# V of a cache group as one load into two neighbouring pages, used behind its own group's K

## The chip, the cores and the metric

The kernel runs on one core of a Trainium2 chip. The metric is the device time of one execution in microseconds (us), the median of several runs. The core has five engines that run side by side and wait for each other through semaphores: TensorE (PE in the profile, its weight loads PEld), VectorE (DVE), ScalarE (ACT), GpSimd (POOL) and SyncE (SP). Here SP issues all large loads, in order, on one queue that is served by 16 DMA engines. On-chip memory has 128 partitions; matmul results go to a separate memory (PSUM, tiles named ps... here).

## What is computed

One decode step: attention of one new token over a long cache (A), a gated feed-forward layer (B), and a gate that mixes them. Cut to what matters, in bf16:

```
Hq, Hkv, Sk, Dh = 32, 8, 32768, 128        # x: (1, 1, 512)
g = sigmoid((x * gate_w).sum(-1))
q = (x @ wq)                               # 32 heads, 4 for each of the 8 K/V groups
scores = q . k * Dh**-0.5                  # 32768 scores for each head
p = softmax(scores);  o = p . v;  a = o @ wo
b = (silu(x @ w_gate) * (x @ w_up)) @ w_down      # inner width 1792
out = g * a + (1 - g) * b
```

The cache is the work: 8 groups of K and V with 32768 rows of 128 bf16 numbers, 8.39 MB each for K and for V, 134 MB in all. Each byte is used once, for 4 heads.

## The kernel before, in words

**Pages.** The cache passes through `page`, five pages of 32 KB per partition (4.19 MB over 128 partitions). A page holds one block: half of K or of V of one group, 16384 rows, 128 to a partition. K block b uses page `PG_K[b]` = 0 or 2, V block b uses `PG_V[b]` = 1 or 3 (L71, L72). Page 4 (`PG_X`) holds wq at the start and wo at the end; page 3 (`PG_F`) first holds the weights w_gate and w_up.

**Loads** (SP, L298 to L348). SP waits until a page is free and issues its load; everything behind it on SP waits too. The order is wq, x, gate_w, w_gate, w_up, K(0,0), K(0,1), V(0,0), K(1,0), V(0,1), K(1,1), and then for each group g from 2 on K(g,0), V(g-1,0), K(g,1), V(g-1,1). So V comes one group after K. A K page is free when TensorE has transposed it (`sem_fill`), a V page when its matmuls are done (`sem_v_free`). V(0,1) waits until the products with w_gate and w_up are done (`sem_pe_h`). At the end come V(7,0), V(7,1), which goes into K's page 0 (L342) so that it need not wait for V(6,1), then w_down in one load and wo in five cuts (8, 10, 8, 4 and 2 of 32 columns).

**TensorE** (L351 on). The loop at L500 runs over nine values of i = 16 g, the last for the V that is left. For a block of K (`emit_k`) it waits for the page and works through eight units. A unit is eight transposes of 128 x 128 fp32 words (`emit_fill`, L408), which VectorE copies back to on-chip memory as ktT (L630), and, two units later, 16 small matmuls that make scores (`emit_scores`, L420). For a block of V (`emit_v`, L465) it waits for the page and for the exps of that block, and does 32 matmuls of 16 columns (4 rows by 4 heads) by 512, spread over four strips of 32 columns of the array, into `ps_o`. The order in one pass is K(g,0), a reduce, V(g-1,0), K(g,1), V(g-1,1). The reduce (`emit_reduce`, L446) sums the strips of the group before that one, out of `acc`.

**The other engines.** When both K blocks of a group are through, VectorE has its maximum over the partition (L635, L637), GpSimd takes it over all partitions (L293), and ScalarE makes the bias (L526) and eight exps (L535, four heads by two blocks) into ET. ScalarE then copies the group before out of `ps_o` into `acc` (L547). ET, `ps_o` and `acc` are single buffers.

**The end** (`emit_end`, L474 to L498, and L673 to L691). Sum of the exps (L477), the last reduce, eight of 14 matmuls with w_down (L205 in `emit_wide`), then o in the shape for wo (L659 to L671), the first cut of wo (L205, eight matmuls), the rest of w_down (six), the second cut (ten), a copy by VectorE (L685), the rest of wo as small matmuls (L217 in `emit_rows`), a copy (L687) and two stores (L244).

Of the kernel before, what the change touches and what calls it, by code (L numbers as in the profile page):

```python
# [13 lines left out]
def bass_gated_mix__gqa_block_cached__swiglu_ffn__decode_kernel(  # L14
# [14 lines left out]
    G = A_k_cache.shape[1]  # L29
# [3 lines left out]
    HPG = H // G  # L33
# [36 lines left out]

    PG_K = (0, 2)  # L71
    PG_V = (1, 3)  # L72
    PG_F = 3
    PG_X = 4
    NPG = 5

    with ExitStack() as es:
        def S_(name):
            return es.enter_context(nc.semaphore(name))

        sem_page = [S_(f"s_page{i}") for i in range(4)]
        sem_q = S_("s_q")
# [112 lines left out]

        def row_view(p):
            return page[:, p, :].rearrange("p (r d) -> p r d", d=DH)

        wq_v = page[:, PG_X, 0 : KC * H * DH].rearrange("p (c n) -> p c n", c=KC)
        wgu = page[:, PG_F, 0 : 2 * KC * F].rearrange("p (w c f) -> p w c f", w=2, c=KC)  # L200
        wo_v = page[:, PG_X, 0 : WOJ * NOUT].rearrange("p (j n) -> p j n", j=WOJ)
# [47 lines left out]
        with nc.Block("main") as block:  # L249
# [47 lines left out]
            @block.sync  # L297
            def _(sp):  # L298
                def cache(which, g, b, p, sem):
                    sp.dma_start(  # L300
                        page[:, p, :].rearrange("p (r d) -> p r d", d=DH),
                        which[0, g, b * BLK : (b + 1) * BLK, :].rearrange("(p r) d -> p r d", r=R),
                    ).then_inc(sem, 16)

                def load_k(g, b):
                    if g:
                        sp.wait_ge(sem_fill, UPG * (g - 1) + UPP * (b + 1))
                    cache(A_k_cache, g, b, PG_K[b], sem_page[PG_K[b]])

                def load_v(g, b):  # L310
                    if g:
                        sp.wait_ge(sem_v_free, NB * (g - 1) + b + 1)
                    elif PG_V[b] == PG_F:
                        sp.wait_ge(sem_pe_h, 1)
                    cache(A_v_cache, g, b, PG_V[b], sem_page[PG_V[b]])

                sp.dma_start(wq_v, A_wq.rearrange("(p c) n -> p c n", c=KC)).then_inc(sem_q, 16)  # L317
                sp.dma_start(x_row[0:1, :], A_x[0, :, :]).then_inc(sem_ld_x, 16)
                sp.dma_start(gw_row[0:1, :], gate_w.unsqueeze(0)).then_inc(sem_ld_x, 16)
                for w, src in enumerate((B_w_gate, B_w_up)):  # L320
                    sp.dma_start(  # L321
                        wgu[:, w, :, :], src.rearrange("(p c) f -> p c f", c=KC)
                    ).then_inc(sem_f, 16)
                for b in range(NB):
                    load_k(0, b)
                load_v(0, 0)
                load_k(1, 0)
                load_v(0, 1)
                load_k(1, 1)
                for g in range(2, G):  # L330
                    for b in range(NB):
                        load_k(g, b)
                        load_v(g - 1, b)

                def load_wo(k):
                    a, b = WO_CUTS[k], WO_CUTS[k + 1]
                    src = A_wo.rearrange("(p j) n -> p j n", j=WOJ)
                    sp.dma_start(wo_v[:, a:b, :], src[:, a:b, :]).then_inc(sem_wo[k], 16)  # L338

                load_v(G - 1, 0)  # L340
                sp.wait_ge(sem_fill, UPG * (G - 1) + UPP)
                cache(A_v_cache, G - 1, 1, PG_K[0], sem_page[PG_K[0]])  # L342
                sp.dma_start(  # L343
                    wd[:, :, :], B_w_down.rearrange("(p j) n -> p j n", j=FC)
                ).then_inc(sem_ld_wd, 16)
                sp.wait_ge(sem_pe_q, 1)
                for k in range(len(sem_wo)):
                    load_wo(k)  # L348

            @block.tensor  # L350
            def _(pe):  # L351
# [77 lines left out]
                def emit_k(i, b):  # L429
                    pe.wait_ge(sem_page[PG_K[b]], i + 16)  # L430
                    for u in range(UPP + LAG):
                        if u >= LAG:
                            pe.wait_ge(sem_cp, i + (UPP * b + u - LAG + 1))
                        if u < UPP:
                            emit_fill(b, u)
                        if u >= LAG:
                            if u == LAG:
                                pe.wait_ge(sem_exp, i + 8 * (b + 1))
                            ins = emit_scores(b, u - LAG)
                    ins.then_inc(sem_sc, 8)  # L440

                def emit_reduce(i):
                    pe.wait_ge(sem_acc, i)
                    pe.wait_ge(sem_rc, i)
                    for q in range(RQ):
# [8 lines left out]

                def emit_v(i, b, pg=None, landed=None):
                    pg = PG_V[b] if pg is None else pg
                    view = row_view(pg)
                    if b == 0:
                        emit_reduce(i)
                    pe.wait_ge(sem_page[pg], i if landed is None else landed)  # L460
                    pe.wait_ge(sem_exp, i + 8 * (b + 1))
                    for k in range(R // RQ):
                        n = b * R + k * RQ
                        c = k % NSTRIP
                        ins = pe.matmul(  # L465
                            ps_o[32 * c : 32 * c + RQ * HPG, :],
                            ET[:, n : n + RQ, :].rearrange("p n h -> p (n h)"),
                            view[:, k * RQ : (k + 1) * RQ, :],
                            start=(b == 0 and k < NSTRIP),
                            stop=(b == NB - 1 and k >= R // RQ - NSTRIP),  # L470
                            skip_group_check=True,
                        )
                    ins.then_inc(sem_v_free, 1)

                def emit_end():
# [7 lines left out]
                    ).then_inc(sem_pe_S, 1)  # L483
                    emit_reduce((G + 1) * STEP)
                    pe.wait_ge(sem_dve_tT, 1)
# [13 lines left out]

                with pe.Fori(0, (G + 1) * STEP, STEP) as i:  # L500
                    for b in range(NB):
                        with pe.If(i < G * STEP):
                            emit_k(i, b)
                            if b:
                                with pe.If(i > 0):
                                    emit_v(i, b)
                        if b == 0:
                            with pe.If(i > 0):
                                emit_v(i, b)
                    with pe.If(i > (G - 1) * STEP):  # L510
                        emit_v(G * STEP, 1, PG_K[0], (G + 1) * STEP)
                        emit_end()

            @block.scalar
            def _(act):
# [8 lines left out]
                def emit_exps(g):  # L524
# [3 lines left out]
                    ).then_inc(sem_nbias, 1)  # L528
                    act.wait_ge(sem_nbias, g + 1)
                    for b in range(NB):  # L530
                        if g:
                            act.wait_ge(sem_v_free, NB * (g - 1) + b + 1)
                        sc = ps_sc[b][:, :].rearrange("p (t h) -> p h t", h=HPG)
# [10 lines left out]
                def emit_acc(g):  # L544
                    act.wait_ge(sem_v_free, NB * (g + 1))
                    act.wait_ge(sem_red, STEP * (g + 1))
# [4 lines left out]
                for g in range(G):  # L551
                    emit_exps(g)
                    if g:
                        emit_acc(g - 1)
                emit_acc(G - 1)

            @block.vector
            def _(dve):
# [8 lines left out]
                dchain(dve.memset(qblk[:, :], 0.0))  # L567
                dve.sem_inc(sem_rc, 2 * STEP)
                dve.wait_ge(sem_pe_x, 1)
# [52 lines left out]
                def copy_red(i, at):  # L622
                    dve.wait_ge(sem_red, i)
                    dve.tensor_copy(oT[:, at], ps_m[:, M_P0 : M_P0 + HPG]).then_inc(sem_rc, STEP)

                with dve.Fori(0, G * STEP, STEP) as i:
# [15 lines left out]
                    )  # L642
                    with dve.If(i > STEP):
                        copy_red(i, bass.ds(i, HPG))

# [4 lines left out]
                dve.memset(ps_w[:, :], 0.0).then_inc(sem_psw, 1)  # L650
                copy_red(G * STEP, slice(G * STEP, G * STEP + HPG))
                dve.wait_ge(sem_pe_S, 1)
# [3 lines left out]
                )  # L656
                copy_red((G + 1) * STEP, slice((G + 1) * STEP, (G + 1) * STEP + HPG))
                dve.wait_ge(sem_rc, STEP * (G + 2))
                dve.tensor_tensor(  # L659
                    oTs[:, :].rearrange("p (g h) -> p g h", h=HPG),  # L660
                    oT[:, 2 * STEP :].rearrange("p (g s) -> p g s", s=STEP)[:, :, 0:HPG],
                    rSg[:, :].rearrange("p (g h) -> p g h", h=HPG),
# [57 lines left out]
```

## Time and profile before

| | us |
|---|---|
| runs, median of 3 (lowest to highest) | 352.46 (352.34 to 352.58) |
| profiled execution, first to last instruction (span) | 350.2 |
| median less span (start and end of an execution) | 2.26 |

| engine | busy us in the span | share |
|---|---|---|
| PE, PEld | 269.0, 230.9 | 77%, 66% |
| DVE | 176.8 | 50% |
| ACT | 32.3 | 9% |
| POOL | 6.9 | 2% |

How to read what follows: a profile page gives, first, such shares; then the span in 40 slices, with a digit for the busy tenths of each slice (9 is 90% or more); then the DMA queues with packets, MB and the share of 16 engines' span that their packets took; then the chain that ended last, which is followed back from the last instruction to what released each step. A row of the timeline has start, length, engine, line, operation, `written<-read`, shape and count, and in brackets the idle time before and what ended it. The granted clock is the share of full speed that TensorE's throttle gave it; its mean over the span is 0.846, and single stretches show 0.50 or 1.00. The page's issue table gives 16 K loads and 16 V loads of 4096 KB, with a median of 27.1 and 31.2 us from issue to landing, nearly all of it spent in the queue behind others.

### The profile page before, as it was taken

To read this page: it belongs to the slowest core of one execution; us is meant where nothing else is said; L and a number is where in the kernel's file an instruction comes from. 1 tells how busy PE (TensorE), PEld (TensorE's weight loads), DVE (VectorE), ACT (ScalarE), POOL (GpSimd) and SP (SyncE) were. 2 spreads that over 40 slices of the span, in tenths; PEclk is the share of its full clock that TensorE was granted. 3 is DMA by queue.
4 is the path that set the end of the run, shared out by engine and by line. 5 is a ranking of instruction groups with operands and counts; after the bars stand their busy time and mean duration, and the time that the engine had idled before them with its cause. 6 is when DMAs were issued, how large, how long until landed. Compare 5 with 4: busy or idle time off the path is not lost.

```text
span 350.2 us, 8919 instructions
## 1 busy us (share of the span) xinstructions
PE 269.0 (77%) x4005; PEld 230.9 (66%) x4005; DVE 176.8 (50%) x193; ACT 32.3 (9%) x148; POOL 6.9 (2%) x29
## 2 busy tenths in 40 slices
PE   0446987799999959897797969694896949795675
PEld 0446987787796939495785839392886849493332
DVE  0111868474783928366382828183473819184011
ACT  1000000500030040002100040004000040004000
POOL 4000000000000000000000000000000000000000
PEclk9999989696998989679696969899698969679565
DMA  8999999999999999999999999999999999999995
GB/s 348 395 453 417 438 445 425 418 419 449 434 430 423 427 446 430 430 423 423 449 430 434 419 434 438 434 430 419 442 438 434 423 423 442 438 434 419 425 415 234
DMA packets 5924, 148.23 MB, mean 423 GB/s; under 512 B 666, under 2 KB 668, under 8 KB 924
## 3 DMA queue, kind: packets, MB, share of 16 engines
q1 hardware_dynamic: 5912, 148.12, 98.6%
q8 instruction: 6, 0.10, 0.1%
q14 instruction: 2, 0.02, 0.0%
q10 hardware_dynamic: 4, 0.00, 0.0%
HBM read 148.11 MB, written 0.00 MB: 423 GB/s over the span
## 4 chain that ended last, share of the span: by engine, by line
DMA 64%; PE 32%; DVE 2%; SPq 1%; issue 1%
DMA page<-in_A_k_cache_dram 53%; PE pst L408 24%; DMA page<-in_A_wo_dram 11%; PE ps_sc L420 5%; DVE ktT L630 1%; PE ps_o L465 1%; PE pst L217 1%; PE pst L205 0%; PE ps_m L446 0%; SPq L321 0%; SPq L300 0%; DVE part L685 0%; SPq L343 0%; SPq L338 0%; SPq L317 0%
## 5 line engine op out<-in xcount | busy, mean ns | idle before, releaser
L630 DVE COPY ktT<-pst 128x2048 bf16<-128x2048 bf16 x128 | 156.1, 1224 | 106.4 <-PE pst L408 99.2
L408 PE MATMUL pst<-ident_f,page 128*128 128x128 f32 x1024 | 158.8, 313 | 40.9 <-DMA page<-in_A_k_cache_dram 35.6
L408 PEld LDWEIGHTS pst<-ident_f,page 128*128 128x128 f32 x1024 | 136.1, 163 | 51.6 <-DMA page<-in_A_k_cache_dram 43.7
L420 PE MATMUL ps_sc<-qcur,ktT 128*128 128x8 bf16 x2048 | 67.8, 166 | 8.6 <-DVE ktT L630 8.6
L420 PEld LDWEIGHTS ps_sc<-qcur,ktT 128*128 128x128 bf16 x2048 | 66.9, 97 | 11.3 <-DVE ktT L630 10.0
L465 PE MATMUL ps_o<-page,ET 128*16 128x512 bf16 x512 | 43.2, 497 | 4.6 <-DMA page<-in_A_v_cache_dram 4.6
L465 PEld LDWEIGHTS ps_o<-page,ET 128*16 128x16 bf16 x512 | 13.5, 105 | 23.8 <-issue 11.9
L526 ACT ACTIVATE nbias<-gmax 128x4 f32<-128x4 f32 x8 | 1.7, 207 | 263.4 <-POOL gmax L293 263.4
L535 ACT ACTIVATE ET<-ps_sc,nbias 128x128 bf16<-128x128 f32 x64 | 24.1, 553 | 0.6
L535 ACT ACTIVATION_READ_ACCUMULATOR ET<-ps_sc,nbias 128x1 f32 x64 | 18.0, 282 | 0.0
L635 DVE TENSOR_REDUCE pmaxf<-ps_sc 128x4 f32<-128x512 f32 x16 | 11.1, 692 | 11.5 <-PE ps_sc L420 11.5
L446 PE MATMUL ps_m<-sel,acc 128*128 128x4 f32 x72 | 10.4, 268 | 3.8 <-ACT acc L547 3.8
L446 PEld LDWEIGHTS ps_m<-sel,acc 128*128 128x128 f32 x72 | 9.8, 211 | 4.4 <-ACT acc L547 4.4
L394 PE MATMUL ps_m<-xT,page 128*128 128x1 bf16 x112 | 6.9, 198 | 5.0 <-DMA page<-in_B_w_up_dram 5.0
L357 PE MATMUL ps_m<-ones_bf,x_row 1*128 1x1 bf16 x4 | 0.3, 172 | 12.9 <-DMA gw_row<-in_gate_w_dram 12.9
L394 PEld LDWEIGHTS ps_m<-xT,page 128*128 128x128 bf16 x112 | 6.8, 159 | 5.1 <-DMA page<-in_B_w_up_dram 5.1
L293 POOL PARTITION_ALL_REDUCE gmax<-pmax x8 | 3.0, 373 | 302.8 <-DVE pmax L637 302.8
L357 PEld LDWEIGHTS ps_m<-ones_bf,x_row 1*128 1x128 bf16 x4 | 0.2, 115 | 12.9 <-DMA gw_row<-in_gate_w_dram 12.9
L547 ACT ACTIVATE acc<-ps_o 128x512 f32<-128x512 f32 x8 | 5.2, 648 | 13.7 <-PE ps_o L465 13.7
L653 DVE RECIPROCAL rS<-pst 128x32 f32<-128x32 f32 x1 | 0.4, 357 | 12.0 <-PE pst L477 12.0
L570 DVE CAST xT<-ps_m 128x4 bf16<-128x4 f32 x1 | 0.2, 162 | 11.8 <-PE ps_m L357 11.8
L609 DVE TENSOR_TENSOR t<-sg,ps_m 128x14 f32<-128x14 f32 x1 | 0.2, 170 | 10.8 <-ACT sg L520 10.8
(65 smaller groups left out, 38.5 us busy)
## 6 DMA issues: line engine op xcount, KB each, us to landing
page<-in_A_k_cache_dram SPq DMA_DIRECT2D x16, 4096.0 KB, 27.1
page<-in_A_v_cache_dram SPq DMA_DIRECT2D x16, 4096.0 KB, 31.2
page<-in_A_wq_dram SPq DMA_DIRECT2D x1, 4096.0 KB, 12.2
page<-in_A_wo_dram SPq DMA_DIRECT2D x2, 1024.0 KB, 38.8
page<-in_B_w_gate_dram SPq DMA_DIRECT2D x1, 1792.0 KB, 15.3
page<-in_B_w_up_dram SPq DMA_DIRECT2D x1, 1792.0 KB, 20.5
wd<-in_B_w_down_dram SPq DMA_DIRECT2D x1, 1792.0 KB, 34.5
page<-in_A_wo_dram SPq DMA_DIRECT2D x1, 1280.0 KB, 39.1
```

What stands on the lines that cost most here:

```text
L217: ins = pe.matmul(ps_c[32 * oc : 32 * oc + (1 if e else SW), 0:128], lhs(e), rhs[:, oc * 128 : (oc + 1) * 128], start=first, stop=last, sk ...
L293: pool.partition_all_reduce(gmax[:, g, :], pmax[:, g * STEP : g * STEP + HPG], 128, ReduceOp.max).then_inc(sem_gmax, 1)
L394: ins = pe.matmul(ps_m[:, base + j : base + j + 1], wgu[:, w, c, :].rearrange("d (p j) -> d j p", j=FC)[:, j, :], xT[:, c : c + 1], start= ...
L408: ins = pe.transpose(pst[u % NST][:, k * 128 : (k + 1) * 128], kv[:, n * 128 : (n + 1) * 128], ident_f[:, :],)
L420: ins = pe.matmul(ps_sc[b][:, col : col + 2 * HPG], kt[:, k, e, :], qcur[:, e, :], start=(e == 0), stop=(e == 1),)
L446: ins = pe.matmul(ps_m[:, M_P0 : M_P0 + HPG], acc[:, q, :], sel4[:, q * HPG : (q + 1) * HPG], start=(q == 0), stop=(q == RQ - 1),)
L465: ins = pe.matmul(ps_o[32 * c : 32 * c + RQ * HPG, :], ET[:, n : n + RQ, :].rearrange("p n h -> p (n h)"), view[:, k * RQ : (k + 1) * RQ, ...
L526: act.activation(nbias[:, g, :], gmax[:, g, :], ACT.Copy, scale=-SCALE).then_inc(sem_nbias, 1)
L535: act.activation(ET[:, b * R : (b + 1) * R, h], sc[:, h, :], ACT.Exp, bias=nbias[:, g, h : h + 1], scale=SCALE, accum_out=esum[:, g, b, h ...
L547: act.activation(acc[:, :, :].rearrange("p q d -> p (q d)"), ps_o[:, :], ACT.Copy).then_inc(sem_acc, STEP)
L630: dve.tensor_copy(ktT[:, u % NKT, :], pst[u % NST][:, :].bitcast(BF16)).then_inc(sem_cp, 1)
L635: dve.tensor_reduce(pmaxf[:, b, :], sc, AX.X, ALU.max).then_inc(sem_pmax, 4)
```

## The change

K's pages become 0 and 1. Pages 2 and 3 become one V buffer of 64 KB per partition, which holds a whole group's V; w_gate and w_up lie at its start first. V of a group is one load of 8.39 MB, issued behind both K loads of the same group, and it waits until the V before has been used up (V of group 0: until w_gate and w_up have). In it a partition holds 256 neighbouring rows. So that scores and V rows stay in step, a K block now takes, of each partition's 256 rows, the first or the second 128: 32 KB out of each 64 KB.

TensorE does K(g,0), K(g,1), reduce of group g-1, V(g) in each of eight passes, with no branches. V waits for all eight exps of its group and is 64 matmuls in a row. ScalarE waits for the V before ahead of all eight exps, and copies `ps_o` to `acc` directly behind a group's exps. VectorE copies the reduce's result in each pass. The end is the same but for the numbering.

The diff, cut to its core:

```diff
-    PG_K = (0, 2)
-    PG_V = (1, 3)
-    PG_F = 3
+    PG_K = (0, 1)
+    PG_V = 2
...
+        v_page = page[:, PG_V : PG_V + NB, :].rearrange("p b e -> p (b e)")
+        v_rows = v_page.rearrange("p (r d) -> p r d", d=DH)
...
                 def load_k(g, b):
                     if g:
                         sp.wait_ge(sem_fill, UPG * (g - 1) + UPP * (b + 1))
-                    cache(A_k_cache, g, b, PG_K[b], sem_page[PG_K[b]])
+                    sp.dma_start(
+                        page[:, PG_K[b], :],
+                        A_k_cache[0, g, :, :].rearrange("(p b r) d -> b p (r d)", b=NB, r=R)[b],
+                    ).then_inc(sem_page[b], 16)
...
+                def load_v(g):
                     if g:
-                        sp.wait_ge(sem_v_free, NB * (g - 1) + b + 1)
-                    elif PG_V[b] == PG_F:
+                        sp.wait_ge(sem_v_free, g)
+                    else:
                         sp.wait_ge(sem_pe_h, 1)
-                    cache(A_v_cache, g, b, PG_V[b], sem_page[PG_V[b]])
+                    sp.dma_start(
+                        v_page, A_v_cache[0, g, :, :].rearrange("(p r) d -> p (r d)", r=NT)
+                    ).then_inc(sem_page[NB], 16)
...
-                for b in range(NB):
-                    load_k(0, b)
-                load_v(0, 0)
-                load_k(1, 0)
-                load_v(0, 1)
-                load_k(1, 1)
-                for g in range(2, G):
+                for g in range(G):
                     for b in range(NB):
                         load_k(g, b)
-                        load_v(g - 1, b)
+                    load_v(g)
...
-                load_v(G - 1, 0)
-                sp.wait_ge(sem_fill, UPG * (G - 1) + UPP)
-                cache(A_v_cache, G - 1, 1, PG_K[0], sem_page[PG_K[0]])
...
+                def emit_v(i):
+                    pe.wait_ge(sem_page[NB], i + 16)
+                    pe.wait_ge(sem_exp, i + 2 * STEP)
+                    for k in range(NT // RQ):
+                        n = k * RQ
...
+                with pe.Fori(0, G * STEP, STEP) as i:
                     for b in range(NB):
...
+                        emit_k(i, b)
+                    emit_reduce(i)
+                    emit_v(i)
+                emit_end()
...
+                    if g:
+                        act.wait_ge(sem_v_free, g)
                     for b in range(NB):
-                        if g:
-                            act.wait_ge(sem_v_free, NB * (g - 1) + b + 1)
...
                 for g in range(G):
                     emit_exps(g)
-                    if g:
-                        emit_acc(g - 1)
-                emit_acc(G - 1)
+                    emit_acc(g)
```

More of the change, by code (lines that the diff above doesn't have):

```diff
@@ L79, in S_ @@
             return es.enter_context(nc.semaphore(name))
-        sem_page = [S_(f"s_page{i}") for i in range(4)]
+        sem_page = [S_(f"s_page{i}") for i in range(3)]
         sem_q = S_("s_q")
@@ L194, in bass_gated_mix__gqa_block_cached__swiglu_ffn__decode_kernel @@
         ps_w = pst[0][:, 512:1024]
-        def row_view(p):
-            return page[:, p, :].rearrange("p (r d) -> p r d", d=DH)
+        v_page = page[:, PG_V : PG_V + NB, :].rearrange("p b e -> p (b e)")
+        v_rows = v_page.rearrange("p (r d) -> p r d", d=DH)
         wq_v = page[:, PG_X, 0 : KC * H * DH].rearrange("p (c n) -> p c n", c=KC)
-        wgu = page[:, PG_F, 0 : 2 * KC * F].rearrange("p (w c f) -> p w c f", w=2, c=KC)
+        wgu = page[:, PG_V, 0 : 2 * KC * F].rearrange("p (w c f) -> p w c f", w=2, c=KC)
         wo_v = page[:, PG_X, 0 : WOJ * NOUT].rearrange("p (j n) -> p j n", j=WOJ)
@@ L298, in _ @@
             def _(sp):
[L299 to L303, printed above, removed]
                 def load_k(g, b):
@@ L307, in load_k @@
                         sp.wait_ge(sem_fill, UPG * (g - 1) + UPP * (b + 1))
-                    cache(A_k_cache, g, b, PG_K[b], sem_page[PG_K[b]])
-                def load_v(g, b):
+                    sp.dma_start(
[3 more added lines that the diff above has]
+                def load_v(g):
                     if g:
-                        sp.wait_ge(sem_v_free, NB * (g - 1) + b + 1)
-                    elif PG_V[b] == PG_F:
+                        sp.wait_ge(sem_v_free, g)
+                    else:
                         sp.wait_ge(sem_pe_h, 1)
-                    cache(A_v_cache, g, b, PG_V[b], sem_page[PG_V[b]])
+                    sp.dma_start(
+                        v_page, A_v_cache[0, g, :, :].rearrange("(p r) d -> p (r d)", r=NT)
+                    ).then_inc(sem_page[NB], 16)
                 sp.dma_start(wq_v, A_wq.rearrange("(p c) n -> p c n", c=KC)).then_inc(sem_q, 16)
@@ L429, in emit_k @@
                 def emit_k(i, b):
-                    pe.wait_ge(sem_page[PG_K[b]], i + 16)
+                    pe.wait_ge(sem_page[b], i + 16)
                     for u in range(UPP + LAG):
@@ L442, in emit_reduce @@
                 def emit_reduce(i):
-                    pe.wait_ge(sem_acc, i)
-                    pe.wait_ge(sem_rc, i)
+                    pe.wait_ge(sem_acc, i + STEP)
+                    pe.wait_ge(sem_rc, i + STEP)
                     for q in range(RQ):
@@ L453, in emit_reduce @@
                     ins.then_inc(sem_red, STEP)
[L455 to L463, printed above, removed]
+                def emit_v(i):
[3 more added lines that the diff above has]
+                        n = k * RQ
                         c = k % NSTRIP
@@ L467, in emit_v @@
                             ET[:, n : n + RQ, :].rearrange("p n h -> p (n h)"),
-                            view[:, k * RQ : (k + 1) * RQ, :],
-                            start=(b == 0 and k < NSTRIP),
-                            stop=(b == NB - 1 and k >= R // RQ - NSTRIP),
+                            v_rows[:, n : n + RQ, :],
+                            start=(k < NSTRIP),
+                            stop=(k >= NT // RQ - NSTRIP),
                             skip_group_check=True,
@@ L483, in emit_end @@
                     ).then_inc(sem_pe_S, 1)
-                    emit_reduce((G + 1) * STEP)
+                    emit_reduce(G * STEP)
                     pe.wait_ge(sem_dve_tT, 1)
@@ L498, in emit_end @@
                         emit_wide(pe, wd, tT, j, False, False)
-                with pe.Fori(0, (G + 1) * STEP, STEP) as i:
+                with pe.Fori(0, G * STEP, STEP) as i:
                     for b in range(NB):
[L502 to L512, printed above, removed]
+                        emit_k(i, b)
+                    emit_reduce(i)
+                    emit_v(i)
+                emit_end()
             @block.scalar
@@ L544, in emit_acc @@
                 def emit_acc(g):
-                    act.wait_ge(sem_v_free, NB * (g + 1))
+                    act.wait_ge(sem_v_free, g + 1)
                     act.wait_ge(sem_red, STEP * (g + 1))
@@ L567, in _ @@
                 dchain(dve.memset(qblk[:, :], 0.0))
-                dve.sem_inc(sem_rc, 2 * STEP)
+                dve.sem_inc(sem_rc, STEP)
                 dve.wait_ge(sem_pe_x, 1)
@@ L622, in copy_red @@
                 def copy_red(i, at):
-                    dve.wait_ge(sem_red, i)
+                    dve.wait_ge(sem_red, i + STEP)
                     dve.tensor_copy(oT[:, at], ps_m[:, M_P0 : M_P0 + HPG]).then_inc(sem_rc, STEP)
@@ L642, in _ @@
                     )
-                    with dve.If(i > STEP):
-                        copy_red(i, bass.ds(i, HPG))
+                    copy_red(i, bass.ds(i, HPG))
                 dve.wait_ge(sem_exp, STEP * (G + 1))
@@ L650, in _ @@
                 dve.memset(ps_w[:, :], 0.0).then_inc(sem_psw, 1)
-                copy_red(G * STEP, slice(G * STEP, G * STEP + HPG))
                 dve.wait_ge(sem_pe_S, 1)
@@ L656, in _ @@
                 )
-                copy_red((G + 1) * STEP, slice((G + 1) * STEP, (G + 1) * STEP + HPG))
+                copy_red(G * STEP, slice(G * STEP, G * STEP + HPG))
                 dve.wait_ge(sem_rc, STEP * (G + 2))
@@ L660, in _ @@
                     oTs[:, :].rearrange("p (g h) -> p g h", h=HPG),
-                    oT[:, 2 * STEP :].rearrange("p (g s) -> p g s", s=STEP)[:, :, 0:HPG],
+                    oT[:, STEP : (G + 1) * STEP].rearrange("p (g s) -> p g s", s=STEP)[:, :, 0:HPG],
                     rSg[:, :].rearrange("p (g h) -> p g h", h=HPG),
```

## The prediction

> **What bounds the kernel now.** I read the page's slices and queue table first, then the chain that ended last, then the timeline of the last 50 us.
>
> ```profile
> DMA  8999999999999999999999999999999999999995
> ...
> q1 hardware_dynamic: 5912, 148.12, 98.6%
> ```
>
> The loads keep the 16 DMA engines busy for 98.6% of the span. The missing 1.4% of 350.2 us is 4.9 us, about what the two ends account for (the first load is issued at 0.74 us, nothing is loaded after 348.1 us). So there is one unbroken stream of 148.12 MB, and nothing between the ends can be won by issuing a load earlier.
>
> The pace of that stream is read where TensorE waits for a K page. These starts are single rows of the timeline (columns: start, length, engine, line, operation; in brackets the idle time before and what ended it):
>
> ```profile
> 246.44 5.38 PE L408 MATMUL pst<-ident_f,page 128*128 128x128 f32 x24 [5.64 <-DMA page<-in_A_k_cache_dram]
> ...
> 304.73 5.38 PE L408 MATMUL pst<-ident_f,page 128*128 128x128 f32 x24 [1.97 <-DMA page<-in_A_k_cache_dram]
> ...
> 318.06 0.56 PE L420 MATMUL ps_sc<-qcur,ktT 128*128 128x8 bf16 x16 [0.54 <-DVE ktT L630]
> 318.54 1.90 PE L465 MATMUL ps_o<-page,ET 128*16 128x512 bf16 x32
> ...
> 323.18 0.30 ACT L535 ACTIVATION_READ_ACCUMULATOR ET<-ps_sc,nbias 128x1 f32 x1
> ...
> 325.64 3.59 PE L465 MATMUL ps_o<-page,ET 128*16 128x512 bf16 x32
> ...
> 333.87 3.59 PE L465 MATMUL ps_o<-page,ET 128*16 128x512 bf16 x32 [4.63 <-DMA page<-in_A_v_cache_dram]
> ...
> 341.17 1.04 PE L205 MATMUL pst<-wd,tT 128*1 128x512 bf16 x6
> 343.74 1.44 PE L205 MATMUL pst<-page,O 128*1 128x512 bf16 x10 [1.54 <-DMA page<-in_A_wo_dram]
> ```
>
> Six pages lie between the K pages that land at 246.4 and 304.7: 58.29 / 6 = 9.715 us for 4.19 MB, or 431.7 GB/s. Three more pages land by 333.83 (29.1 us, the same pace). What is left then is w_down and wo, 6.03 MB, and the chain shows that they set the end:
>
> ```profile
> 304.59 39.11 DMA page<-in_A_wo_dram
> 343.70 0.04 issue
> 343.74 1.46 PE pst L205 x10
> ...
> 348.12 0.43 PE pst L217 x4
> 348.55 0.02 issue
> 348.58 0.29 DVE res_row L687
> ```
>
> So the end is the last byte of wo plus 0.5 us of rows and the store. Ahead of it TensorE has little room: it is ready for wo's second cut at 342.21 (341.17 + 1.04), and that cut lands at 343.70. **The room in the tail is 1.5 us.** That is the number this change has to be held against.
>
> **Part by part.**
>
> *The stream's bytes and order.* The same 32 pages are loaded, in the order K, K, V, V instead of K and V in turn. K of group 7, block 0 is now the 29th page; block 1 was the 29th before, at 304.73. Both leave three pages to come, so V of group 7 is complete at 333.83 as before, w_down and wo as before. This needs the queue never to run dry, which is checked below.
>
> *Pieces of 64 KB.* A V page was 128 pieces of 32 KB; now 128 pieces of 64 KB make two pages. The tail bounds what a piece costs. Its 6.03 MB arrive in 768 pieces (48 per engine) in 348.08 - 333.83 = 14.25 us. At 431.7 GB/s they would take 13.97 us with 11.5 pieces of 32 KB per engine. So 0.28 us / 36.5 = 7.7 ns a piece. V loses 1024 of 2048 pieces, 64 per engine: -0.49 us. If the queue cuts 64 KB into two again, 0. I take -0.43 us, the 7 groups of V ahead of the last K, as nothing shows a cut.
>
> *Half as many V loads.* The queue table leaves no gap to save at a load's start or end (4.9 us over everything, ends included), so I take 0. The Trainium skill ("DMA: Bandwidth & Descriptors", Anatomy of one DMA) gives a fixed 2.0 us for each load beside its bytes. Taken as time of the stream, 8 loads fewer would be an estimated 16 us; here it would make a page 11.6 us, and the rows show 9.715, so loads queued behind each other hide it.
>
> *Where the pages lie in HBM.* K is now 32 KB of every 64 KB, V 64 KB per partition; before, all pages were contiguous, partitions 32 KB apart. No row has this pitch. The nearest is wo, 2 to 10 KB out of every 32 KB, which runs at 6.03 MB / 14.25 us = 423 GB/s, all of it explained by pieces in the line above. I take 0; each 1% of the stream's pace would be 3.1 us (32 x 9.715 / 100). The Trainium skill (same page, Latency and other measured facts) speaks against the change: copies lose speed at power-of-two row pitches, 207 GB/s at 512 KiB where 214 is full. An estimated 3% here would be some 10 us; no run here shows such a pitch, and 64 KB is an eighth of it.
>
> *V follows its own group on TensorE.* This is the costly part. Before, V of group g-1 ran between the K blocks of group g, and its exps had been ready for long; at the end only 32 matmuls waited for the last page. Now each group is serial: K block 0, K block 1, maximum and exps, 64 V matmuls. The pieces, from rows:
> - a K block, start to end of its scores: 11.95 us (227.02 to 238.97, at full clock), 13.05, 13.55, 13.89 (304.73 to 318.62), 14.0 us (246.44 to 260.45). Directly behind another K block there is one row: 46.15 to 59.79, 13.64 us, 0.70 of them "issue". I take 13.5 for block 0 and 13.0 for block 1; bounds 11.95 and 13.9.
> - scores to last exp: 318.62 to 323.48, 4.9 us (278.93 to 283.84 in the group before: the same). The reduce (1.03 us, L446) now stands in this gap and is hidden.
> - V: 32 matmuls take 1.90 us at granted clock 1.00 and 3.59 at 0.50; so 64 take 3.8 to 7.2. All waits of 2.7 us and more ahead of TensorE work end in 0.50 (263.2 to 265.9, 320.5 to 324.0, 329.2 to 333.9), and the clock came back to 1.00 at 337.6, after 3.7 us of V. So I take one half slow and one fast: 3.59 + 1.90 = 5.5.
>
> The tail, then: 304.73 + 13.5 + 13.0 = 331.2; + 4.9 = 336.1 (V landed at 333.83 and now waits for the exps); + 5.5 = 341.6, where V ended at 337.46 before. From V's end to ready for wo's second cut took 4.75 us (to 342.21): 346.35, later than its landing. From that cut's start to the last row took 343.74 to 348.55 = 4.81 us, of which 0.57 were waits for cuts 3 and 4 (the timeline shows 0.27 and 0.30), which have landed by then: 4.24. End 350.6 instead of 348.55: **+2.05 us**.
>
> *What waits behind what.* SP's queue is in order: V(g+1) waits for V(g) to be used up, and behind it stand both K loads of group g+2. If V(g) lands at T, its K block 0 landed at T - 29.1; scores end at T - 2.6, exps at T + 2.3, V at T + 7.8. The queue then still holds K of group g+1, until T + 19.4: 11.6 us in hand. In group 0 the exps also have a table load of 1.28 us (L535), they end at 66.0, V at 71.5, and the queue lasts to 81.0: 9.5 us. K block 1 is asked for when its predecessor's last transposes are done, at T - 4.4, with all of the next block 0 still to come: 14 us. V of group 0 waits for the gate and up products (L394, done at 29.65) and holds K of group 1 behind it on SP; the queue is full until 42.2. On ACT, acc(g) now precedes exps(g+1), which come 30 us later. On DVE the copy of the reduce follows the maximum, off the path. All this costs 0. TensorE has 13.5 + 13.0 + 4.9 + 5.5 = 36.9 us of chain in a group of 4 x 9.715 = 38.9.
>
> *Loop.* Fewer branches and eight fewer issues of 0.33 us on SP, none of them on the path: 0.
>
> **Sum.** Tail +2.05, pieces -0.43: +1.6 us. The profiled execution spans 350.2 us; the runs' median lies 2.26 us above the span, and I carry that: 350.2 + 1.6 + 2.26 = **354.1 us**.
>
> **Rivals.**
> 1. *The tail stays hidden.* All clocks good: 304.73 + 2 x 11.95 + 4.9 = 333.5, V starts on landing at 333.87 and takes 3.8, to 337.7: no later than before by more than the 1.5 us in hand. It decides when V ends before 339.0. Then only the pieces count: 352.46 - 0.49 = 352.0, not slower. For it: one row at 11.95. Against it: four of five rows are over 13, and idle time ahead of V is certain.
> 2. *TensorE's chain becomes the bound.* Slow rows throughout: 13.9 + 13.64 + 4.9 + 7.2 = 39.6 against 38.9, 0.8 us a group, 7 groups, 5.5 us; with the worst tail (+4.8) 362.8. It decides when a group takes over 38.9 us. Against it: the sum of middling rows is 2 us below.
> 3. *The pitch slows the stream* by 1%: 354.1 + 3.1 = 357.2, and 3 us more for each further per cent; the rule cited above is of this kind.
> 4. *The stream gets quicker* than the pieces explain, by 0.5%: 1.6 us, with a hidden tail 350.9. No row speaks for it.
>
> **Chances.** A measurement of this kernel can tell about 0.2% (0.7 us) from no change. Forecast (late by 0.7 to 4.8 us) 0.55; hidden tail 0.22; quicker stream 0.10; TensorE as the bound 0.07; pitch 0.06. So slower 0.68, the same 0.22, faster 0.10. The range runs from 351.8, which takes in the hidden tail, to 357.0: the worst tail with slow V and no saving by pieces is 304.73 + 13.9 + 13.64 + 4.9 + 7.2 + 4.75 + 4.24 = 353.4, +4.8 us, or 357.3, hardly all at once.
>
> **What would show it.** After: DMA share near 98.6% until the last wo; K of group 7, block 0 near 304.3; the last V's first matmul waiting for exps, not for its load; V ending near 341; no wait on wo's last cuts. Wrong if V waits for the load (rival 1), K starts without waiting for loads in the later groups (rival 2), pages land more than 9.8 us apart (rival 3), or the queue runs dry between V's end and the next V.

## The result

The changed kernel takes 350.83 us (median of 6 runs, 350.74 to 350.98), the kernel before beside it 352.12 (6 runs, 351.58 to 352.58): ratio 0.9965, 95% interval 0.9953 to 0.9976. A repeat on another chip gave 350.96 (12 runs) against 351.63 (35 runs), 0.9985 (0.9975 to 0.9996). So it is 0.7 to 1.3 us **faster**, 0.2 to 0.4%: a small gain, but clear of both intervals. The forecast was 1.6 us slower, 354.1. Three of the six runs of the kernel before, 352.34 to 352.58, are those of the table ahead of the prediction; the other three took 351.58 to 351.91. The profiled execution spans 349.6 us, 0.6 less than before.

The page of the changed kernel, its slices and its queue:

```profile
DMA  8999999999989999999999999999999998999995
...
q1 hardware_dynamic: 4760, 148.12, 98.6%
```

The same bytes come in 1152 fewer packets (5912 before), and the share is the same 98.6%: the stream is still unbroken, with one V buffer. 1024 of the packets are V's pieces, so 64 KB stays whole; the other 128 are completions of the 8 loads that went.

The tail, TensorE's rows of the timeline:

```profile
304.26 1.97 PE L397 MATMUL pst<-ident_f,page 128*128 128x128 f32 x16 [3.21 <-DMA page<-in_A_k_cache_dram]
...
316.06 1.95 PE L397 MATMUL pst<-ident_f,page 128*128 128x128 f32 x16
...
327.84 1.03 PE L435 MATMUL ps_m<-sel,acc 128*128 128x4 f32 x8
333.39 5.13 PE L450 MATMUL ps_o<-page,ET 128*16 128x512 bf16 x64 [4.52 <-DMA page<-in_A_v_cache_dram]
...
342.05 0.60 PE L204 MATMUL pst<-wd,tT 128*1 128x512 bf16 x6
343.18 0.81 PE L204 MATMUL pst<-page,O 128*1 128x512 bf16 x10 [0.53 <-DMA page<-in_A_wo_dram]
...
347.57 0.23 PE L216 MATMUL pst<-page,O2z 128*32 128x128 bf16 x1 [0.16 <-DMA page<-in_A_wo_dram]
```

K of group 7 lands at 304.2, as forecast (304.3). Its blocks then take 11.9 and 11.8 us instead of 13.5 and 13.0; the exps are ready in time, and V waits for its load, not for them. V ends at 338.5, TensorE is ready for wo's second cut at 342.65 and waits 0.53 us for it, and for the last cut as well. The chain that ended last runs through wo's last landing, 0.55 us earlier than before (347.53 for 348.08). First the end of the chain, then the row of the kernel before that shows its last landing, a weight load of TensorE (PEld) that waited for it:

```profile
303.85 43.69 DMA page<-in_A_wo_dram
...
347.57 0.32 PE pst L216 x4
...
347.92 0.29 DVE res_row L661
```

```profile
348.12 0.10 PEld L217 LDWEIGHTS pst<-page,O2z 128*32 128x32 bf16 x1 [0.30 <-DMA page<-in_A_wo_dram]
```

The copy of the result row (res_row) starts 0.66 us earlier: 0.55 by the landing, and 0.11 because the last four matmuls take 0.32 us instead of 0.43.

What differs most is the clock. Busy time and granted clock in stretches of the tail (columns: stretch, length, then busy us and count of PE, PEld, DVE, ACT, POOL, then the clock, the DMA share and GB/s), first the changed kernel, then the kernel before:

```profile
340.00:342.00 2.00, 1.42 (x20) 0.63 (x24) 0.88 (x5) 0.00 (x0) 0.00 (x0) 1.00 0.98 410
...
344.00:346.00 2.00, 0.74 (x32) 0.47 (x36) 0.69 (x1) 0.00 (x0) 0.00 (x0) 1.00 0.85 332
346.00:348.00 2.00, 1.00 (x48) 0.48 (x34) 0.08 (x1) 0.00 (x0) 0.00 (x0) 1.00 0.17 61
```

```profile
338.00:340.00 2.00, 1.59 (x16) 1.07 (x16) 1.13 (x5) 0.16 (x1) 0.00 (x0) 1.00 1.00 420
340.00:342.00 2.00, 1.45 (x15) 0.42 (x15) 0.35 (x3) 0.00 (x0) 0.00 (x0) 0.80 1.00 421
342.00:344.00 2.00, 0.46 (x6) 0.10 (x8) 0.00 (x0) 0.00 (x0) 0.00 (x0) 0.50 0.98 409
344.00:346.00 2.00, 1.21 (x14) 0.16 (x9) 0.69 (x1) 0.00 (x0) 0.00 (x0) 0.50 0.96 387
346.00:348.00 2.00, 2.00 (x56) 1.47 (x56) 0.00 (x0) 0.00 (x0) 0.00 (x0) 0.50 0.31 121
```

The rows behind wo's second cut, which the prediction priced from the second table at half clock, run at full clock in the first. In the kernel before the clock had come back behind the last V (at 337.6) and fell again at about 341.2, although TensorE had not waited longer than 0.46 us at a time in between.

### The profile page after: what moved, and what is told of

Same layout as the page of the kernel before. It is cut to its first block, busy times and chain, and to the rows that moved or that the text cites. A ratio compares the mean times of both kernels' runs of the same rounds, so it can differ in the third digit from the quotient of the medians.

```text
span 349.6 us, 8827 instructions
## 1 busy us (share of the span) xinstructions
PE 253.9 (73%) x4005; PEld 215.2 (62%) x4005; DVE 176.0 (50%) x194; ACT 33.3 (10%) x148; POOL 6.9 (2%) x29
## 3 DMA queue, kind: packets, MB, share of 16 engines
q1 hardware_dynamic: 4760, 148.12, 98.6%
## 5 line engine op out<-in xcount | busy, mean ns | idle before, releaser
L397 PE MATMUL pst<-ident_f,page 128*128 128x128 f32 x1024 | 144.4, 292 | 28.9 <-DMA page<-in_A_k_cache_dram 24.8
L397 PEld LDWEIGHTS pst<-ident_f,page 128*128 128x128 f32 x1024 | 120.9, 150 | 35.2 <-DMA page<-in_A_k_cache_dram 28.4
L450 PE MATMUL ps_o<-page,ET 128*16 128x512 bf16 x512 | 45.1, 529 | 33.8 <-ACT ET L513 24.8
L450 PEld LDWEIGHTS ps_o<-page,ET 128*16 128x16 bf16 x512 | 15.4, 116 | 60.2 <-ACT ET L513 34.5
L611 DVE TENSOR_REDUCE pmaxf<-ps_sc 128x4 f32<-128x512 f32 x16 | 11.1, 691 | 11.9 <-PE ps_sc L409 11.9
L383 PE MATMUL ps_m<-xT,page 128*128 128x1 bf16 x112 | 6.9, 198 | 4.9 <-DMA page<-in_B_w_up_dram 4.9
L359 PE MATMUL ps_m<-xT,page 128*128 128x1 bf16 x128 | 3.6, 165 | 0.3 <-DVE gwT L547 0.3
## 6 DMA issues: line engine op xcount, KB each, us to landing
page<-in_A_wq_dram SPq DMA_DIRECT2D x1, 4096.0 KB, 12.5
```

What stands on the lines that cost most here:

```text
L359: ins = pe.matmul(ps_m[:, M_Q0 + h : M_Q0 + h + 1], wq_v[:, c, h * DH : (h + 1) * DH], xT[:, c : c + 1], start=(c == 0), stop=(c == KC - 1),)
L383: ins = pe.matmul(ps_m[:, base + j : base + j + 1], wgu[:, w, c, :].rearrange("d (p j) -> d j p", j=FC)[:, j, :], xT[:, c : c + 1], start= ...
L397: ins = pe.transpose(pst[u % NST][:, k * 128 : (k + 1) * 128], kv[:, n * 128 : (n + 1) * 128], ident_f[:, :],)
L450: ins = pe.matmul(ps_o[32 * c : 32 * c + RQ * HPG, :], ET[:, n : n + RQ, :].rearrange("p n h -> p (n h)"), v_rows[:, n : n + RQ, :], start ...
L611: dve.tensor_reduce(pmaxf[:, b, :], sc, AX.X, ALU.max).then_inc(sem_pmax, 4)
```

## The experiments

Theory: the gain is the pieces of the stream, and the longer chain of V costs nothing because it fits the room in the tail. Rivals: the gain comes from the quicker tail; or from fewer loads; or from where the pages lie in HBM, the memory that the cache is loaded from. Then: which step of the tail's sum was wrong, the chain ahead of V's end or the room behind it.

### The pieces

**V in 32 KB pieces**, one load, contiguous blocks:

```diff
-   page[:, PG_K[b], :], A_k_cache[...].rearrange("(p b r) d -> b p (r d)", ...)[b]
+   page[:, PG_K[b], :], A_k_cache[...].rearrange("(b p r) d -> b p (r d)", ...)[b]
-   v_page, A_v_cache[0, g, :, :].rearrange("(p r) d -> p (r d)", r=NT)
+   page[:, PG_V : PG_V + NB, :], A_v_cache[0, g, :, :].rearrange("(b p r) d -> p b (r d)", ...)
```

> The changed kernel, but V of a group (still one load into one buffer) lies in HBM as two blocks, so that each partition gets two pieces of 32 KB instead of one of 64 KB; K blocks are contiguous again. Pieces theory (the gain is the 64 fewer pieces per DMA engine, 7.7 ns each by the prediction's tail): the stream is 0.5 us longer again, last cut of wo lands near 348.0 instead of 347.5, time near 351.3 us. Tail theory (the gain is TensorE at full clock behind the last load, pieces cost nothing): unchanged, 350.8 us. Loads theory (the gain is 8 loads fewer, each with a start or an end): unchanged, 350.8 us.

Measured: 351.58 us (11 runs; before 351.60), ratio 1.0005 (0.9991 to 1.0019). The gain is gone, +0.6 us on the changed kernel's 350.96 (with the kernel before at 351.6 beside both); wo lands 0.39 us later than with 64 KB (347.92).

**K and V in 16 KB pieces**: the same two rearrangements with `j` = 4 places of 64 rows for each partition of a group.

> The changed kernel with all of K and V in pieces of 16 KB (four places of HBM for each partition of a group): 8192 pieces instead of 3072, 320 more on each DMA engine. Pieces theory at 7.7 ns: the stream is 2.5 us longer, time 353.3 us. Tail and loads theories: unchanged, 350.8 us.

Measured: 353.85 us (6 runs), ratio 1.0072 (1.0052 to 1.0092), +2.9 on the changed kernel for 320 pieces more on each engine: 9 ns a piece. The queue table of its profile points the same way:

```profile
q1 hardware_dynamic: 9880, 148.12, 98.9%
```

98.9% of 16 x 352.6 us less 98.6% of 16 x 349.6 is 64 us of packets for 5120 packets more, 12.5 ns each (the rounding of the shares allows 11.4 to 13.7). That is more than the 9 ns by which the end moves; no run explains the difference. The direction goes with the pieces, and the size is near theirs; the tail and loads theories forecast no change here.

**V in two loads**, the second edit above replaced by a loop over b with `page[:, PG_V + b, :]`, 32 KB of every 64 KB, and a semaphore each:

> The changed kernel with V of a group as two loads, issued one behind the other, each of 32 KB out of every 64 KB of a partition, with the same buffer and the same order of work. Pieces theory: like one load in 32 KB pieces (which gave 351.6), so 0.5 to 0.8 us over the changed kernel. If the number of loads has a price of its own, more than that one, by 8 starts.

Measured: 351.67 us (11 runs), ratio 1.0011 (0.9995 to 1.0027). It is 0.7 us over the changed kernel beside it, and within 0.1 us of the one load in 32 KB pieces. Eight loads more cost nothing that shows.

**The pitch alone**, the kernel before with one edit:

```diff
-   which[0, g, b * BLK : (b + 1) * BLK, :].rearrange("(p r) d -> p r d", r=R)
+   which[0, g, :, :].rearrange("(p b r) d -> b p r d", b=NB, r=R)[b]
```

> The kernel before with one edit: each K and V block takes 32 KB out of every 64 KB of HBM for a partition instead of contiguous 4 MB. Same pieces, same order. Pieces theory: no change, 351.6 us. Pitch theory (the place in HBM changes the stream's pace): 1% would be 3.1 us either way.

Measured: 351.70 us (11 runs; before 351.63), ratio 1.0005 (0.9996 to 1.0014). A pitch of 64 KB costs less than 0.15%. The Trainium skill's loss at large power-of-two row pitches ("DMA: Bandwidth & Descriptors", Latency and other measured facts) does not reach down to this pitch, for these loads; larger pitches were not tried.

**The control**, the changed kernel itself:

> The changed kernel itself, as the control for the kernels beside it: 350.8 us, and the kernel before at 351.6, so that the ratio is near 0.998.

Measured: 350.96 us, as told above; 11 of 12 runs lie between 350.80 and 351.26, one took 352.82. Its profile is worth more than its time, for TensorE was slower in it than in the first:

```profile
333.91 6.16 PE L450 MATMUL ps_o<-page,ET 128*16 128x512 bf16 x64 [4.03 <-ACT ET L513]
...
344.51 0.81 PE L204 MATMUL pst<-page,O 128*1 128x512 bf16 x10 [0.30 <-PEq L248]
...
347.61 0.23 PE L216 MATMUL pst<-page,O2z 128*32 128x128 bf16 x1 [0.25 <-DMA page<-in_A_wo_dram]
```

Here V does wait for the exps, ends at 340.1, and the second cut is taken 1.4 us after it had landed (it had by 343.14 in the first profile; PEq in the row is TensorE's own sequencer). The last cut is waited for all the same, and the span is 349.6 again. So the room does not end at the second cut: behind it lie waits for later cuts (0.48, 0.70 and 0.16 us in the first profile), and they take up a delay as well.

### The clock and the room in the tail

**More reduces at the end**, 2 and 5 more (`emit_reduce(G * STEP, 3)` and `(G * STEP, 6)`, which repeat the four matmuls):

> The changed kernel with the last reduce done three times over: 2 x 1.03 = 2.1 us more of TensorE between the last V and the second cut of wo. The profile of the changed kernel shows TensorE waiting 0.5 us for the second cut and 1.3 us in all for the three after it, so 1.9 us of room. Hidden-tail theory: +0.2 us, 351.0. If the tail is on the path already: +2.1 us, 352.9.

> The same with the last reduce done six times over: 5 x 1.03 = 5.2 us more. Hidden-tail theory with 1.9 us of room: +3.3 us, 354.1. If there were no room: +5.2 us, 356.0. If there were as much room as 5 us: no change, 350.8.

Measured: 354.23 us (7 runs, 352.2 to 356.4), ratio 1.0059 (1.0038 to 1.0079), and 357.5 (five of six runs, 356.4 to 358.1; the sixth took 361.8), 1.0165 (1.0146 to 1.0183): +3.3 and +6.6 on the changed kernel's 350.96. Both are more than the work added (2.1 and 5.2), so no theory of room alone fits. The profile of the first one shows what came on top; it is of the slowest of the seven runs (356.44), so the others lost less:

```profile
342.10 3.42 PE L435 MATMUL ps_m<-sel,acc 128*128 128x4 f32 x24 [0.42 <-ACT acc L525]
345.45 1.02 PE L204 MATMUL pst<-wd,tT 128*1 128x512 bf16 x8
```

```profile
342.00:344.00 2.00, 1.90 (x17) 1.90 (x18) 0.32 (x2) 0.05 (x1) 0.00 (x0) 1.00 1.00 413
344.00:346.00 2.00, 2.00 (x17) 1.54 (x16) 0.31 (x2) 0.00 (x0) 0.00 (x0) 0.54 0.84 329
346.00:348.00 2.00, 1.72 (x21) 0.48 (x15) 0.58 (x4) 0.00 (x0) 0.00 (x0) 0.50 0.13 48
```

TensorE is busy for 3.9 of 4 us and loses its clock all the same, at about 344.2, some 2 us into the reduces. From there on everything runs at half clock (1.02 us for eight wide matmuls that took 0.60). V ended at 341.3 here, and from there to the last row it is 12.1 us, or 9.8 without the 2.4 us of added reduces: near the forecast's 9.0. So a late V with a tail at half clock, as the prediction had it, does occur. These two edits changed two things at once, the length of the tail and its clock.

**The gap filled**, 32 transposes of a constant between reduce and V, in the idle time before the exps (a helper in the kernel, written out here):

```diff
                     emit_reduce(i)
+                    for _ in range(32):
+                        pe.transpose(ps_o[:, 0:128], ident_f[:, :], ident_f[:, :])
                     emit_v(i)
```

> The changed kernel with 32 idle-time transposes of a constant (3.7 us at full clock) between the reduce and V of each group, where TensorE waits for the exps; their result is overwritten or multiplied by zero. Clock theory (the half clock of V and of the K blocks is what the idle time in front of them brings): V's 64 matmuls 3.8 us instead of 5.0 to 6.5, K blocks near 11.9 us, granted clock over 0.93, less spread; the time stays at the stream's 350.8 us or falls by 0.2. If low use and not idle time cools TensorE, V stays at 5 us or more.

Measured: 351.01 us (11 runs), ratio 0.9990 (0.9974 to 1.0006): the changed kernel's time.

```profile
329.76 3.69 PE L446 MATMUL ps_o<-ident_f 128*128 128x128 f32 x32
333.93 3.63 PE L454 MATMUL ps_o<-page,ET 128*16 128x512 bf16 x64 [0.48 <-ACT ET L518]
...
343.21 0.81 PE L204 MATMUL pst<-page,O 128*1 128x512 bf16 x10 [1.52 <-DMA page<-in_A_wo_dram]
```

V takes 3.6 us in every group instead of 5.0 to 6.5, so the wait in front of it was what slowed it. The room at the second cut is 1.5 us. None of it shows in the time, so V's end was not on the path; the quicker-tail rival is out, but for the 0.11 us behind the last landing. The profile's granted clock is only 0.916, not over 0.93. K of group 7 still begins at half clock (4.51 us for its first 24 transposes), after 1.95 us of idle time. And in five of the eight groups the filler itself takes 5.2 to 6.5 us instead of 3.69, because the clock had already fallen: in group 1 it fell at 96.5, in the reduce, with no wait over 0.54 us in the 20 us before, and came back at 103.3, after 5.4 us of nothing but transposes.

**V's end put where the prediction had it**: the same kernel with 19 and 34 transposes between the last V and the last reduce.

> The kernel with the filled gap, with 19 more transposes of a constant (2.2 us at full clock, 1.8 us of it beyond ScalarE's copy) between the last V and the last reduce: as if V had ended at 339.4 instead of 337.6. The prediction put the point from which the tail decides at 339.0 and counted 4.24 us from wo's second cut to the last row: by it +0.4 us or more, 351.4 and up. By the profiles since (the second cut waited for nothing with V's end at 340.1, and the last cut was still waited for by 0.25 us) there is room to 340.3: no change, 351.0.

> The same with 34 transposes (3.9 us, 3.6 beyond the copy): as if V had ended at 341.2, where the prediction had put it. By the prediction's tail +1.6 us over the kernel with the filled gap, 352.6. By the room to 340.3: +0.9 us, 351.9.

Measured: 351.25 us (12 runs), ratio 0.9987 (0.9975 to 1.0000), and 351.16 (8 runs, of which three took 354.5 to 354.6), 1.0019 (0.9985 to 1.0053). The first lies between its two expectations, 351.0 and 351.4; the kernel before took 351.79 beside it, 0.16 more than beside the filled gap. The profile of the second, timeline and then the end of its chain:

```profile
337.78 3.93 PE L466 MATMUL pst<-ident_f 128*128 128x128 f32 x34
...
341.69 1.03 PE L435 MATMUL ps_m<-sel,acc 128*128 128x4 f32 x8
...
345.35 0.81 PE L204 MATMUL pst<-page,O 128*1 128x512 bf16 x10 [0.30 <-PEq L248]
```

```profile
345.35 0.83 PE pst L204 x10
...
346.21 0.70 DVE part L666
...
346.95 1.23 PE pst L216 x60
...
348.20 0.29 DVE res_row L668
```

The transposes end at 341.7, but ScalarE's copy of `ps_o`, for which the last reduce waits otherwise, ran beside them. The reduce starts 3.4 us later than in the kernel with the filled gap (341.69 for 338.31), where V ended at 337.56: it is as if V had ended at 340.9, close to the prediction's 341.2 (341.6 less 0.43). Now TensorE is the chain, the second cut is taken 2.2 us after it landed, and res_row starts at 348.20: 0.13 us after that of the kernel with the filled gap (348.07, its last rows at clock 0.50) and 0.28 after that of the changed kernel, not 1.6. From that end of V to the last row it is 4.4 us to the second cut and 2.8 behind it, 7.2 in all, at clock 1.00, where the prediction had 4.75 + 4.24 = 9.0. Both expectations of +0.9 us and more were too high for the run profiled and for the median. The three runs of 354.5 and more are 3.4 us up. Their mean granted clock, 0.913 to 0.918 against 0.921 to 0.932 in the other five, fits an estimated 8 us at half clock (a mean lower by 0.011 over 350 us, at a loss of 0.5); no profile of such a run was taken, so that their tail lost the clock is argued, not shown.

**A longer chain in each group but the last**: 34 transposes behind V in groups 0 to 6, so that the tail stays.

> The changed kernel with 34 transposes (3.9 us) behind V in groups 0 to 6, so that only the chain of the groups gets longer and the tail does not. With the prediction's blocks (13.5, 13.0, 4.9, 5.5) a group would take 40.8 us against 38.8 of the stream, K would fall behind by 2 us a group and the end by up to 12 us. With the measured ones (11.9 to 13.0, 11.8 to 12.9, 4.9, 5 to 6.2) a group takes 37.5 to 40: mostly hidden, K starts up to 1 us late now and then, 350.9 to 351.5.

Measured: 351.15 us (12 runs, 350.6 to 353.3), ratio 0.9990 (0.9977 to 1.0004).

```profile
300.98 3.93 PE L446 MATMUL pst<-ident_f 128*128 128x128 f32 x34
304.74 1.91 PE L397 MATMUL pst<-ident_f,page 128*128 128x128 f32 x16
```

K of group 7 no longer waits for its load and starts at 304.74, 0.5 us later than in the changed kernel; the end does not move. So with 3.9 us added TensorE has just used up what it had to spare in a group, some 3.4 us and not the 2.0 of the prediction.

## Why the prediction was wrong, point by point

- **What bounds the kernel: right.** One unbroken stream, whose last byte sets the end. Only pieces moved the time, as long as the tail kept its clock; the two kernels with more reduces, and three runs of the one with 34 transposes, are those that left the stream's time clearly.
- **Queue depth, single V buffer: right.** SP's waits never ran it dry (98.6%), even with 3.9 us more in each group (98.7%).
- **Pieces: right mechanism, sized a little low.** 7.7 ns a piece and -0.43 to -0.49 us were forecast; 9 ns and 0.55 us (landing of wo), 0.6 to 0.7 us (against 32 KB pieces) came out. Half as many loads 0, pitch 0: right. The fixed 2.0 us that the prediction takes from the Trainium skill ("DMA: Bandwidth & Descriptors", Anatomy of one DMA) stands there for loads that GpSimd issues. SP issues them here, and no run shows the figure.
- **The tail, +2.05 us: wrong, and this is the step that failed.** Two terms of it. *The chain up to V's end*: K blocks of 13.5 and 13.0 us were taken from rows most of which begin at half clock, behind a wait. The prediction's reading that waits of 2.7 us and more end in 0.50 does not carry over either: in the changed kernel K of groups 4 and 7 starts at full clock behind waits of 3.51 and 3.21 us. Now block 1 follows block 0 directly, and its first transposes are at full clock in 6 of 8 groups (1.95 us for 16; 4.5 for 24 in the other two). In the two profiles the pair took 23.7 and 24.7 us instead of 26.5, and V ended at 338.5 and 340.1 instead of 341.2. *From V's end to the last row*, the larger one: 4.75 and 4.24 us were carried over from the old tail. All of the 4.24, and the last 1.0 of the 4.75, were taken at clock 0.50 there. With V's end moved to 340.9, the two took 4.4 and 2.8 us, 7.2 instead of 9.0, and the end moved by 0.13 to 0.28 us. So even the first term, had it been right, would have cost next to nothing, as long as the tail kept its clock. Why it falls at 341.2 in the kernel before and holds in the changed one stays open.
- **"The room in the tail is 1.5 us": too small.** It was measured at wo's second cut alone; the sum took in 0.57 us of later waits, the bound of 339.0 in rival 1 did not. The control, with V's end at 340.1, took that cut 1.4 us late and still waited for the last one.
- **The 2.26 us between span and time: wrong by 1.0 us.** The prediction took it from one execution. In the six runs of the changed kernel it is 1.27 to 1.38. In 79 runs of the kernel before that stood beside the experiments it is 1.3 to 1.6 in 67 and 1.9 to 2.6 in 12, while all their spans are 350.1 to 350.6. So of the 3.3 us between forecast and result, 2.2 are in the span (351.8 for 349.6), nearly all of it the tail, and 1.0 is this term.
- **Rival 1 (the tail stays hidden)** is what happened, at 351 rather than 352.0 us, nearly all of the difference being that last term. What the 0.9965 has beyond 0.7 us fits the same term (the profiled run of the kernel before has 2.26 us of it), but the spans of the other five runs of that kernel are not on record, and what lengthens the time outside the span is not known. Rivals 2, 3 and 4 did not occur.

The Trainium skill ("TensorE: Matmul & The Clock Gate", Part 1) has the full clock come back after one sustained busy window of about 3.4 us, and go after an idle one. The profile before agrees with the first half in the last V (full clock 3.7 us into it), but not in the reduce and V ahead of it: there TensorE is busy for all of 324.2 to 329.2, and the clock stays at 0.50. Nor do the added reduces agree with the second half: the clock had come back at 340.7 and fell at 344.2, with TensorE busy for 3.1 us of these 3.5. The measurement decides: what holds the clock is not how busy the row looks. Each of these stretches holds a reduce, though not every reduce costs the clock (the last one of the changed kernel does not), and the transposes at the end kept it in the run profiled. That the four columns of the reduce's matmuls are the reason is argued, not shown.

## What to carry to other kernels

When a change moves work on TensorE, its durations from the old profile carry the old clock with them: price each moved piece, and all that follows it, at both clocks, and ask what stands in front of it after the change. Room in a tail is the sum of the waits on the path to the end, not the first of them. Take what lies outside the span from many runs, not from one. And where a saturated queue set the time here, each piece that went from a DMA engine's share was worth about 9 ns, while the number of loads and their order showed no price.

## What had not been expected of the hardware

- In a stretch of four-column fp32 matmuls, back to back, the granted clock fell from 1.00 to 0.50 while TensorE shows 3.9 of 4 us busy (the kernel with two more reduces). The transposes used as filler kept it at 1.00 at the end (34 in 3.93 us) and brought it back where it had fallen in a reduce (after 5.4 us).
- Pieces of 64 KB go as one packet each (4760 packets, 5784 with V in pieces of 32 KB), and the step from 32 KB still saves 0.6 to 0.7 us in 351.
